# Attention with a state, then a Mish feed-forward layer: another order of loads, words and state products in the first of eight batches

## The chip, the cores and the metric

One core of a Trainium2 chip. The time is device microseconds of one execution; 706.59 us is the median of three runs. The engines are TensorE (PE), VectorE (DVE), ScalarE (ACT), GpSimd (POOL) and SyncE (SP); each runs its own instructions in order, and they wait for each other through semaphores. SP's instructions here are the issues of DMAs.

## The reference

Inputs: x of 8 batches x 8 heads x 512 tokens x 64, state of 8 x 8 x 32 x 64, and the layer's weights w_in (512 x 2048) and w_out (2048 x 512), both of them 64-bit floats in memory, two words of 32 bits for each value.

```python
scores = scale * x @ state.T            # per batch and head
a = softmax(scores); xread = a @ state
a2 = softmax(scale * state @ x.T); sread = a2 @ x
y = concat([xread, sread], axis=2)      # (8, 8, 544, 64)
y = y.transpose(0, 2, 1, 3).reshape(8 * 544, 512)
h = y @ w_in                            # (4352, 2048)
g = h * tanh(softplus(h))               # Mish
return g @ w_out                        # (4352, 512)
```

## The kernel before, in words

The rows of x are never multiplied by w_in as they stand. As xread is a @ state, the kernel forms state @ w_in for a batch (a *state product*, `sw_slice`, L351: 32 small matmuls for 128 columns), and multiplies the attention weights by that (the *first products*, `gemm1`, L387). Each float32 operand of a large matmul is split into a rounded high part and the rest (`hi`, `lo`; `swh`, `swl`; `gh`, `gl`), and three matmuls are done for one. Mish follows (`take_g`, L373), the split of its result (`split_g`, L377), and the *second products* with w_out (`gemm2`, L441), 24 matmuls of 128x128 by 512 columns, summed in four PSUM accumulators.

The work of a batch is cut into eight slots j = 0 to 7 (loop at L526), each with two 128-wide blocks of the 2048 columns. In slot j: first products j (12 matmuls), Mish j, the state product of slot j + 1, and the second products of an earlier slot, taken from the list `pending` by `second` (L522). Between these, pieces of the next batch's attention are taken from `todo` (L519).

Batch 0 has to bring the weights in as well. They are loaded in eight blocks each: `("i", e)` is block e of w_in, 1 MB in two DMAs (`load_w_in`, L96), `("o", j)` block j of w_out, also 1 MB in two (`load_w_out`, L114). All go through SP's queue, kept in the order of the calls by `load` (L473). A block of w_in waits for one of two raw buffers, which the join of the block before last frees; the load of x for batch 1 goes to the tile that holds x of batch 0 and waits for its last reader, `sread` (L303). The two words of each value are turned into a float32 in three steps: ACT scales the words (`scale_words`, L81: two instructions for w_in, one for w_out, where POOL does the other; block 0 of w_out has both on ACT), DVE joins them (`join_words`, L91), and for w_out DVE splits the result in high and low (`split_w_out`, L127). Mish and the function that scales the words (L87) lie in different tables of ACT, so that a table load of ACT stands between them.

The order on each engine is written down by hand with `behind` (L159): the instructions in the block come after the marked ones on the same engine, and on that engine only; where nothing is marked, a scheduler orders by its own estimate. The marks are entries of `last`, such as "PE", "words", "join", "mish", "swh", "swl". `fill` (L209) issues matmuls whose result nobody reads; each shows as two records in the profile. `FILL` (L28) holds three counts: ahead of state product 0 (L494), ahead of the transposes of the softmax (L502), and after state product 1 (L571).

In the rows, `wir` is a raw block of w_in, `wor` one of w_out, `swp` a state product, `ph` the first products, `acc` the second products (or, from L212, the filler), `ah` and `al` the split attention weights, `e` an exponential, `bd` a copy of the state blocks, `xTp` transposes of x.

Of the kernel before, what the change touches and what calls it, by code (L numbers as in the profile page):

```python
# [24 lines left out]
W = 1024  # L25
LAG = 2
WARM = 10
FILL = 24, 16, 4  # L28


def as_f32(ap):
    return ap.bitcast(F32)
# [7 lines left out]
def state_attention_mish_kernel(ctx, tc, x, state, w_in, w_out, out):  # L40

    nc = tc.nc
# [21 lines left out]
    wo = {}  # L64
# [16 lines left out]
    def scale_words(raw, pool_rounds=False):  # L81

        lw, hw = raw[..., 0], raw[..., 1]
        y = hw.bitcast(F32)
        if pool_rounds:
            nc.gpsimd.tensor_scalar(lw, lw, 0.876 * 2.0 ** -29, 0.49, ALU.mult, ALU.add)
        last["words"] = nc.scalar.activation(y, y, AF.Prelu, scale=2.0 ** -112, alpha=-2.0 ** 32)  # L87
        if not pool_rounds:
            last["words"] = nc.scalar.activation(lw, lw, AF.Copy, scale=0.876 * 2.0 ** -29, bias=0.49)  # L89

    def join_words(raw, to):  # L91
        lw, hw = raw[..., 0], raw[..., 1]
        last["join"] = nc.vector.scalar_tensor_tensor(
            to.bitcast(U32), hw, 3, lw, ALU.logical_shift_left, ALU.bitwise_or)
# [27 lines left out]
    def join_w_out(j, raw):  # L122
        w = pool.tile([P, 2, DM], F32, tag="wt", name=f"w_{j}", bufs=1)
        join_words(raw, w)
        return w

    def split_w_out(j, w):  # L127
        wo[j] = const.tile([P, 2, 2, DM], F32R, tag=f"wo{j}", name=f"wo_{j}")
        nc.vector.tensor_copy(wo[j][:, :, 1], w)
        last["wo"] = nc.vector.tensor_sub(wo[j][:, :, 0], w, as_f32(wo[j][:, :, 1]))  # L130
# [25 lines left out]
    last = {}  # L156

    @contextmanager
    def behind(*marks):  # L159

        with ExitStack() as st:
            for m in marks:
                st.enter_context(tc.issue_after(last[m].ins if hasattr(last[m], "ins") else last[m]))
            yield
# [10 lines left out]
    def attention(b, xs, sn):  # L175
# [75 lines left out]
        def wide(a):  # L251
            return a.unsqueeze(2).to_broadcast([P, 16, NS])

        def groups(a):
            return a.rearrange("p (g n) -> p g n", n=NS)
# [23 lines left out]
        def soft1_a():  # L279
            for kc in two:  # L280
                sm, r1 = small["s1"][kc], small["r1"][kc]
                nc.vector.tensor_reduce(sm, groups(e1[kc]), AX.X, ALU.add)
                nc.vector.tensor_scalar_add(sm, sm, 1e-9)
                nc.vector.reciprocal(r1, sm)
                nc.vector.tensor_mul(groups(e1[kc]), groups(e1[kc]), wide(r1))
            for kc in two:
                if b == 0:
                    at = ps_acc.tile([P, 512], F32, tag="acc", name=f"at_{b}_{kc}")
                    transposed(at, e1[kc])
                else:  # L290
                    at = temp(f"at_{b}_{kc}")
                    nc.vector.transpose(at, e1[kc])
                hi = pool.tile([P, S], F32R, tag=f"ah{kc}", name=f"ah_{b}_{kc}")
                lo = pool.tile([P, S], F32R, tag=f"al{kc}", name=f"al_{b}_{kc}")
                nc.scalar.copy(hi, at)
                last[b, "DVE"] = nc.vector.tensor_sub(lo, at, as_f32(hi))  # L296
                aT[kc] = (hi, lo)

# [28 lines left out]
        if b == 0:  # L327
            first = [lambda: (xt(0), xt(1), xt(2), xt(3), s_(), soft1_e()), soft1_a]
            fills.append(fill)
            rest = [  # L330
                lambda: (soft2_m(0), soft2_m(1)),
                lambda: (soft2_e(0), soft2_e(1)),
                lambda: (e2t(0), e2t(1)),
                lambda: (sr(0), sr(1)),
                lambda: sreadT(),
            ]
# [40 lines left out]
    def split_g(key, g):  # L377
        gh = pool.tile([P, W], F32R, tag="gh", name=f"gh_{key}")
        gl = pool.tile([P, W], F32R, tag="gl", name=f"gl_{key}")
        nc.vector.tensor_copy(gh, g)  # L380
        last["gl"] = nc.vector.tensor_sub(gl, g, as_f32(gh))  # L381
        return gh, gl
# [15 lines left out]
            phs.append(ph)  # L398
        return phs

    def mish(b, j, phs):
        g = new_g(f"{b}_{j}")
        for k, ph in enumerate(phs):
            take_g(g, k, ph)
        return split_g(f"{b}_{j}", g)


    def load_w_s(j):
# [61 lines left out]
    first, rest, aT = attention(0, xs0, sn0)  # L470
    raws, rawo = {}, {}

    def load(*what):  # L473
        for k, i in what:
            with behind("load"):
                if k == "i":
                    raws[i] = load_w_in(i)
                else:
                    rawo[i] = load_w_out(i)
# [5 lines left out]
            else:  # L485
                make_w_out(i, rawo.pop(i))

    load(("i", 0), ("o", 0), ("i", 1), ("o", 1))
    first[0]()
    with behind((0, "scs"), (0, "sub")):  # L490
        make(("i", 0))
    new_accs(0, NT)
    with behind("PE"):
        fills[0](FILL[0], accs[0][NT - 1])  # L494
    with behind((0, "exp")):
        scale_words(rawo[0])
    with behind("PE", "words"):
        sw_next = sw_slice(0, 0, P)
    with behind("swh"):
        scale_words(raws[1])  # L500
    with behind("PE"):
        fills[0](FILL[1], accs[0][NT - 1])  # L502
    with behind("PE", "words"):
        first[1]()
    load(("i", 2), ("o", 2), ("i", 3))
    with behind((0, "DVE")):
        join_w_in(1, raws.pop(1))
        w_0 = join_w_out(0, rawo[0])

    slots = []  # L510
    for b in range(B):
# [10 lines left out]
    def second(ts=None, keep=False):  # L522
        k_, fcs, g_, nt = pending[0] if keep else pending.pop(0)
        gemm2(k_, list(fcs), g_[0], g_[1], nt, ts)

    for n, (key, j) in enumerate(slots):  # L526
        if key == "s":
            if j == 0:
                ws_next = load_w_s(0)
            ws, ws_next = ws_next, load_w_s(j + 1) if j + 1 < 4 else None  # L530
            g = gemm1_s(j, ws)
            pending.append((key, (2 * j, 2 * j + 1, 2 * j + 8, 2 * j + 9), g, 2))
            second()
            continue
        if j == 0 and key > 0:
            aT = nxt_aT
        if key + 1 < B and j == (3 if key == 0 else 0):
            _, pcs, nxt_aT = attention(key + 1, xs_next, sn_next)
            todo += pcs
        phs = gemm1(key, j, aT, sw_next)  # L540
        if (key, j) == (0, 0):
            with behind("PE"):
                sw_next = sw_slice(0, 1, P)
            with behind("swl"):
                split_w_out(0, w_0)
            rawo.pop(0)
            with behind("swh", "wo"):
                g = mish(key, j, phs)
        else:
            g = mish(key, j, phs)  # L550
        pending.append((key, (j, j + 8), g, NT))
        if key == 0 and j + 1 < SLOTS:


            if j == 1:
                with behind("PE"):
                    second((0, 1), True)
            if j:
                with behind("PE"):
                    sw_next = sw_slice(0, j + 1, P)  # L560
            if j == 1:
                with behind("mish", "gl", "swh", "swl"):
                    rest[1]()
            with behind("mish", "gl", "swh", "swl", (0, "exp2") if j else "mish"):
                make(*makes.get(j, ()))
            if j == 0:
                with behind("join"):
                    rest[0]()
            if j == 0:
                with behind("PE"):  # L570
                    fills[0](FILL[2], accs[0][NT - 1])  # L571
                load(*((k, i) for i in range(3, 6) for k in "io" if (k, i) != ("i", 3)))
                with behind("load"):
                    xs_next, sn_next = load_x(1), load_state(1)
                load(*((k, i) for i in range(6, 8) for k in "io"))
            elif j == 1:
                with behind("PE"):
                    second((2, 3))
            elif j == 3:

                for do in (lambda: second((0, 1), True), todo.pop(0), lambda: second((2, 3))):
                    with behind("PE"):
                        do()
            elif j < 6:
                with behind("PE"):
                    second()
        else:
            nb, nj = (key, j + 1) if j + 1 < SLOTS else (key + 1, 0)
            if nb < B and nj % 2 == 0:
                sw_next = sw_slice(nb, nj)  # L590
        for _ in range((0, 0, 1, 1)[j] if key == 0 and j < 4 else 1 + (key == 0)):
            if todo:
                with behind(*(("PE",) if key == 0 and j == 2 else ())):
                    todo.pop(0)()
        if j == SLOTS - 1 and 0 < key + 2 < B:
            with behind("mish"):
                xs_next, sn_next = load_x(key + 2), load_state(key + 2)
        if len(pending) > LAG:
            second()
# [26 lines left out]
```

## Time and profile before

| | us |
|---|---|
| Median of three runs | 706.59 (706.54 to 710.52) |
| The profiled execution, whole | 707.5 |
| Its span, first to last instruction | 705.5 |
| PE busy in the span | 690.3 |
| ACT busy | 277.7 |
| DVE busy | 317.9 |

The span is what the profile's views cut up; the whole execution is 2.0 us longer, and 0.9 us above the median. An engine's busy time counts instructions that run, not those that wait; the idle time in brackets behind a row is the wait of that engine just ahead of it, and the arrow names what ended it.

### The profile page before, as it was taken

The numbers are of one execution on the slowest core, as the hardware profiler recorded it, in microseconds if no ns is written. First come the engines' busy times: TensorE is split into PE (matmuls) and PEld (weight loads), VectorE is DVE, ScalarE is ACT, GpSimd is POOL, SyncE is SP. The second block draws the span as 40 slices with busy tenths as digits, with TensorE's granted clock in tenths as the row PEclk, the third lists the DMA queues.
The fourth block names the chain that finished last, engine by engine and source line by source line (L and its number), as shares of the span: only waits on it lengthen the run. The fifth ranks groups of instructions, "written<-read, shape, count | busy, mean of one in ns | idle before, by whom it ended". The sixth has DMA issues, their size and how long they took to land.

```text
span 705.5 us, 11227 instructions
## 1 busy us (share of the span) xinstructions
PE 690.3 (98%) x4852; PEld 538.4 (76%) x4852; DVE 317.9 (45%) x493; ACT 277.7 (39%) x442; POOL 10.6 (1%) x13
## 2 busy tenths in 40 slices
PE   8889899999999999999999999999999999999997
PEld 7766676777777777777877777777777788977785
DVE  2697595283238323552346333732356324433221
ACT  5697755352236312551246123531247123222110
POOL 0111010000000000000000000000000000000000
PEclk9999999999999999999999999999999999999999
DMA  9997933000210011001010101001010007001001
GB/s 235 256 235 184 230 78 121 6 1 3 66 60 0 2 60 35 31 1 60 7 61 1 35 26 60 1 1 60 1 61 1 1 1 178 3 0 31 1 1 60
DMA packets 32305, 39.78 MB, mean 56 GB/s; under 512 B 5376, under 2 KB 25856, under 8 KB 32256
## 3 DMA queue, kind: packets, MB, share of 16 engines
q1 hardware_dynamic: 31824, 38.97, 21.1%
q8 instruction: 38, 0.62, 0.4%
q10 hardware_dynamic: 432, 0.10, 0.1%
q14 instruction: 11, 0.09, 0.0%
HBM read 25.95 MB, written 8.91 MB: 49 GB/s over the span
## 4 chain that ended last, share of the span: by engine, by line
PE 87%; DMA 5%; ACT 4%; DVE 3%; issue 1%; SPq 0%; ACTq 0%; DVEq 0%
PE acc L451 47%; PE ph L397 23%; PE swp L358 5%; DMA wir<-in_moe_w_in_dram 4%; PE ph_s L429 3%; PE acc_s L451 3%; PE xTp L184 2%; PE srp L308 1%; PE sc L197 1%; PE e2p L240 1%; DMA sn<-in_state_dram 1%; ACT wir L89 1%; ACT wor L87 1%; ACT L375 1%; ACT g L375 0%
## 5 line engine op out<-in xcount | busy, mean ns | idle before, releaser
L451 PE MATMUL acc<-wo,gh 128*128 128x512 f32 x1024 | 326.1, 400 | 0.0
L451 PEld LDWEIGHTS acc<-wo,gh 128*128 128x128 f32 x1024 | 188.4, 188 | 53.6 <-issue 13.5
L451 PE MATMUL acc<-wo,gl 128*128 128x512 f32 x512 | 200.8, 396 | 0.0
L375 ACT ACTIVATE g<-ph 128x512 f32<-128x512 f32 x128 | 74.3, 598 | 189.1 <-DVE gl L381 120.4
L380 DVE CAST gh<-g 128x1024 fp32r<-128x1024 f32 x64 | 44.9, 702 | 168.4 <-PE acc L451 144.9
L451 PEld LDWEIGHTS acc<-wo,gl 128*128 128x128 f32 x512 | 96.3, 188 | 23.2 <-issue 1.2
L397 PE MATMUL ph<-ah,swh 128*128 128x512 f32 x256 | 101.1, 396 | 3.2 <-ACT g L375 1.6
L397 PE MATMUL ph<-al,swh 128*128 128x512 f32 x256 | 101.8, 398 | 0.0
L397 PE MATMUL ph<-ah,swl 128*128 128x512 f32 x256 | 100.0, 393 | 0.0
L381 DVE TENSOR_TENSOR gl<-g,gh 128x1024 fp32r<-128x1024 f32 x64 | 78.3, 1224 | 4.8 <-DVE gh L380 0.5
L370 DVE TENSOR_TENSOR swl<-swp,swh 128x512 fp32r<-128x512 f32 (+1 forms) x72 | 43.0, 627 | 62.1 <-ACT swh L369 62.1
L397 PEld LDWEIGHTS ph<-ah,swh 128*128 128x128 f32 x256 | 48.0, 188 | 16.3 <-ACT g L375 1.8
L397 PEld LDWEIGHTS ph<-al,swh 128*128 128x128 f32 x256 | 48.1, 188 | 11.0 <-DVE al L296 0.4
L397 PEld LDWEIGHTS ph<-ah,swl 128*128 128x128 f32 x256 | 48.1, 188 | 10.0
L369 ACT CAST swh<-swp 128x512 fp32r<-128x512 f32 (+1 forms) x72 | 35.7, 545 | 25.9 <-PE swp L358 25.9
L358 PE MATMUL swp<-w_in_sb,bd 64*32 64x256 f32 (+1 forms) x1152 | 40.8, 358 | 2.1 <-DVE rs L229 2.0
L358 PEld LDWEIGHTS swp<-w_in_sb,bd 64*32 64x32 f32 x1152 | 18.5, 106 | 20.3 <-issue 10.6
L375 ACT ACT_TABLE_LOAD x20 | 25.7, 1283 | 14.9 <-DVE sm L227 6.2
L187 ACT COPY xT<-xTp 128x512 f32<-128x512 f32 x32 | 18.1, 590 | 33.5 <-PE xTp L184 33.2
L460 ACT COPY o<-acc 128x512 f32<-128x512 f32 x16 | 9.4, 587 | 44.8 <-PE acc L451 26.2
L426 DVE TENSOR_TENSOR wl<-ws,wh 128x512 fp32r<-128x512 f32 x16 | 11.1, 692 | 26.6 <-PE ph_s L429 19.8
L458 DVE COPY o<-acc 128x512 f32<-128x512 f32 x16 | 11.0, 688 | 26.4 <-DMA out_dram<-o 13.9
(79 smaller groups left out, 547.3 us busy)
## 6 DMA issues: line engine op xcount, KB each, us to landing
x<-in_x_dram SPq DMA_DIRECT2D x32, 256.0 KB, 3.7
wir<-in_moe_w_in_dram SPq DMA_DIRECT2D x16, 512.0 KB, 10.9
wor<-in_moe_w_out_dram SPq DMA_DIRECT2D x16, 512.0 KB, 13.7
out_dram<-o SPq DMA_DIRECT2D x32, 256.0 KB, 2.4
ws<-w_in_sb SPq DMA_DIRECT2D x16, 256.0 KB, 5.2
sn<-in_state_dram SPq DMA_DIRECT2D x21, 32.0 KB, 3.0
out_dram<-o_s SPq DMA_DIRECT2D x8, 64.0 KB, 1.8
sn<-in_state_dram ACTq DMA_DIRECT2D x3, 32.0 KB, 3.3
```

What stands on the lines that cost most here:

```text
L184: nc.tensor.transpose(pt[:, i * P:(i + 1) * P], xs[:, c, i // 2, (i % 2) * P:(i % 2 + 1) * P], ident)
L187: nc.scalar.copy(xTs[c], pt)
L358: last["PE"] = nc.tensor.matmul(pw[r][o, kc * n:(kc + 1) * n], bds[b][half(r), kc ^ r, o], w_in_sb[half(r), kc * NC + c, j * P:j * P + n], ...
L369: last["swh"] = nc.scalar.copy(hr, pr)
L370: last["swl"] = nc.vector.tensor_sub(lo[:, r].rearrange("p k f -> p (k f)"), pr, as_f32(hr))
L375: last["mish"] = nc.scalar.activation(g[:, k * 512:(k + 1) * 512], ph, AF.Mish)
L380: nc.vector.tensor_copy(gh, g)
L381: last["gl"] = nc.vector.tensor_sub(gl, g, as_f32(gh))
L397: last["PE"] = nc.tensor.matmul(ph, l, r, start=(i == 0), stop=(i == len(seq) - 1))
L426: nc.vector.tensor_sub(lo, w, as_f32(hi))
L429: nc.tensor.matmul(ph[r][:, k * 256:(k + 1) * 256], l[:, c], srT[i][:, c], start=(c == 0 and n == 0), stop=(c == NC - 1 and n == 2))
L451: last["PE"] = nc.tensor.matmul(accs[key][t], g[:, sl], wo[fc % 8][:, fc // 8, w, :], start=(fc == 0 and n == 0), stop=(fc == NFC - 1 and ...
```

## The change

Six edits, all of them in batch 0:

1. The fill counts go from 24, 16 and 4 to 12, 6 and 4.
2. The first loads go i0, i1, o0, o1 rather than i0, o0, i1, o1. Further on, x and state of batch 1 are loaded ahead of o5 rather than behind it.
3. ACT scales the words of o0 not ahead of state product 0 but behind the casts of the attention weights; DVE joins and splits o0 directly behind that.
4. In slot 0, Mish comes behind the words of o0 on ACT, and the casts of state product 1 come behind Mish; the split of Mish's result comes behind them. Before, the casts came first and then Mish.
5. In slots 2, 4, 5 and 6 the second products are cut in halves (tokens 0, 1 and 2, 3), with the state product between them, as in slots 1 and, in part, 3 before. Slot 6 now issues second products of its own.
6. In slot 1 the exponentials of the transposed softmax (`rest[1]`) come behind the words and joins of i3 and o2, not ahead of them.

```diff
-FILL = 24, 16, 4
+FILL = 12, 6, 4
...
-                nc.scalar.copy(hi, at)
+                last[b, "ACT"] = nc.scalar.copy(hi, at)
...
-    def mish(b, j, phs):
+    def take(b, j, phs):
         g = new_g(f"{b}_{j}")
         for k, ph in enumerate(phs):
             take_g(g, k, ph)
-        return split_g(f"{b}_{j}", g)
+        return g
...
-    load(("i", 0), ("o", 0), ("i", 1), ("o", 1))
+    load(("i", 0), ("i", 1), ("o", 0), ("o", 1))
...
-    with behind((0, "exp")):
-        scale_words(rawo[0])
-    with behind("PE", "words"):
+    with behind("PE", (0, "exp")):
         sw_next = sw_slice(0, 0, P)
...
-    with behind((0, "DVE")):
+    with behind((0, "ACT"), (0, "DVE")):
         join_w_in(1, raws.pop(1))
-        w_0 = join_w_out(0, rawo[0])
+        scale_words(rawo[0])
+        w_0 = join_w_out(0, rawo.pop(0))
+        split_w_out(0, w_0)
...
         if (key, j) == (0, 0):
-            with behind("PE"):
+            with behind("words"):
+                g_0 = take(key, j, phs)
+            with behind("PE", "mish", "wo"):
                 sw_next = sw_slice(0, 1, P)
             with behind("swl"):
-                split_w_out(0, w_0)
-            rawo.pop(0)
-            with behind("swh", "wo"):
-                g = mish(key, j, phs)
+                g = split_g(f"{key}_{j}", g_0)
         else:
-            g = mish(key, j, phs)
+            g = split_g(f"{key}_{j}", take(key, j, phs))
...
-            if j == 1:
+            if j and j != 3:
                 with behind("PE"):
                     second((0, 1), True)
...
-            if j == 1:
-                with behind("mish", "gl", "swh", "swl"):
-                    rest[1]()
-            with behind("mish", "gl", "swh", "swl", (0, "exp2") if j else "mish"):
+            with behind("mish", "gl", "swh", "swl"):
                 make(*makes.get(j, ()))
-            if j == 0:
-                with behind("join"):
-                    rest[0]()
+            if j < 2:
+                with behind("join", "words"):
+                    rest[j]()
...
-                load(*((k, i) for i in range(3, 6) for k in "io" if (k, i) != ("i", 3)))
+                load(("o", 3), ("i", 4), ("o", 4), ("i", 5))
                 with behind("load"):
                     xs_next, sn_next = load_x(1), load_state(1)
-                load(*((k, i) for i in range(6, 8) for k in "io"))
-            elif j == 1:
-                with behind("PE"):
-                    second((2, 3))
+                load(("o", 5), ("i", 6), ("o", 6), ("i", 7), ("o", 7))
...
-            elif j < 6:
+            else:
                 with behind("PE"):
-                    second()
+                    second((2, 3))
```

## Rows read from the trace of the kernel before

**Rows 1.** The page: its first part (busy time and share of the span of each engine, whole run) and, from its second part, the DMA engines' busy share in 40 slices of the span.

```profile
PE 690.3 (98%) x4852; PEld 538.4 (76%) x4852; DVE 317.9 (45%) x493; ACT 277.7 (39%) x442; POOL 10.6 (1%) x13
...
DMA  9997933000210011001010101001010007001001
```

**Rows 2.** The view: stretches of the span, in us. Columns: from:to and length, busy time (and instructions) of PE, PE's weight loads, DVE, ACT and POOL, then the granted TensorE clock, the DMA share and GB/s.

```profile
3.00:57.00 54.00, 48.62 (x438) 38.82 (x437) 37.47 (x53) 40.57 (x56) 5.65 (x4) 1.00 1.07 251
...
40.00:50.00 10.00, 7.98 (x65) 6.15 (x64) 9.26 (x15) 9.93 (x15) 2.26 (x1) 1.00 1.08 233
...
57.00:62.00 5.00, 5.00 (x82) 3.89 (x81) 2.02 (x5) 3.64 (x4) 1.12 (x1) 1.00 0.19 45
...
125.00:690.00 565.00, 565.00 (x3828) 441.29 (x3827) 232.09 (x367) 191.64 (x323) 0.00 (x0) 1.00 0.09 27
```

**Rows 3.** The view: TensorE's instructions from 0 to 125 us, grouped by line. Columns: line, engine, operation, tiles, shapes, count, busy us and mean ns, then the idle time ahead of them in us and what released them.

```profile
L397 PE MATMUL ph<-ah,swh 128*128 128x512 f32 x40 | 16.2, 409 | 3.2 <-ACT g L375 1.6 <-ACT swh L369 1.3 <-ACT ah L295 0.2
...
L212 PE MATMUL acc<-xT 128*128 128x128 f32 x88 | 10.5, 277 | 0.0
...
L358 PE MATMUL swp<-w_in_sb,bd 64*32 64x128 f32 (+1 forms) x288 | 8.7, 287 | 2.1 <-DVE rs L229 2.0
...
L184 PE MATMUL xTp<-ident,x 128*128 128x128 f32 x36 | 5.5, 280 | 2.0 <-DVE bd L151 1.6 <-ACT xT L187 0.2
```

**Rows 4.** The view: TensorE in order of time. Columns: start and length in us, engine, line, operation, tiles, shapes, count of records merged into the row, and in brackets the idle time ahead and its releaser.

```profile
1.36 4.64 PE L171 MATMUL warm<-ident 128*128 128x128 f32 x20 [1.36 <-POOL ident masks.py:199]
...
13.33 5.52 PE L212 MATMUL acc<-xT 128*128 128x128 f32 x48
...
19.38 3.84 PE L212 MATMUL acc<-xT 128*128 128x128 f32 x32
...
24.33 0.73 PE L397 MATMUL ph<-ah,swh 128*128 128x512 f32 x2 [0.24 <-ACT ah L295]
...
30.91 0.50 PE L397 MATMUL ph<-ah,swh 128*128 128x512 f32 x1 [1.61 <-ACT g L375]
...
36.67 0.67 PE L358 MATMUL swp<-w_in_sb,bd 64*32 64x128 f32 x32
...
45.09 0.67 PE L358 MATMUL swp<-w_in_sb,bd 64*32 64x128 f32 x32 [2.02 <-DVE rs L229]
...
51.37 0.39 PE L397 MATMUL ph<-ah,swh 128*128 128x512 f32 x1
...
55.14 0.69 PE L358 MATMUL swp<-w_in_sb,bd 64*32 64x128 f32 x32
...
67.61 0.50 PE L397 MATMUL ph<-ah,swh 128*128 128x512 f32 x1 [1.35 <-ACT swh L369]
...
94.59 0.67 PE L358 MATMUL swp<-w_in_sb,bd 64*32 64x128 f32 x32
```

**Rows 5.** The view: ScalarE and then VectorE in order of time, columns as in the group before.

```profile
12.34 1.16 ACT L87 ACTIVATE wir<-wir 128x1024 f32<-128x1024 f32 x1
...
21.19 1.16 ACT L87 ACTIVATE wir<-wir 128x1024 f32<-128x1024 f32 x1 [1.00 <-DMA wir<-in_moe_w_in_dram]
...
23.69 1.07 ACT L295 CAST ah<-at 128x512 fp32r<-128x512 f32 x2 [0.31 <-PE at L259]
...
28.30 0.65 ACT L369 CAST swh<-swp 128x256 fp32r<-128x256 f32 x2 [3.54 <-PE swp L358]
...
30.26 1.09 ACT L375 ACTIVATE g<-ph 128x512 f32<-128x512 f32 x2
...
41.55 1.15 ACT L87 ACTIVATE wir<-wir 128x1024 f32<-128x1024 f32 x1
...
58.35 1.28 ACT L87 ACT_TABLE_LOAD   x1 [1.44 <-DMA wir<-in_moe_w_in_dram]
...
74.28 1.15 ACT L87 ACTIVATE wir<-wir 128x1024 f32<-128x1024 f32 x1 [2.48 <-DMA wir<-in_moe_w_in_dram]
...
15.49 1.22 DVE L93 SCALAR_TENSOR_TENSOR w_in_sb<-wir 128x1024 uint32<-128x1024 uint32 x1
...
18.31 1.28 DVE L285 TENSOR_TENSOR e<-e,r 128x512 f32<-128x512 f32 x2
...
30.10 1.22 DVE L130 TENSOR_TENSOR wo<-w,wo 128x1024 fp32r<-128x1024 f32 x1
...
78.74 0.42 DVE L151 COPY bd<-st 128x256 f32<-128x256 f32 x1
...
87.40 1.25 DVE L93 SCALAR_TENSOR_TENSOR w_in_sb<-wir 128x1024 uint32<-128x1024 uint32 x1 [3.98 <-ACT wir L89]
```

**Rows 6.** The view: the loads. First three rows: SyncE's queue in order of time (start, length of the issue, both halves of a load together). Then two rows of the DMA issues, of the stretches 17.7 to 17.9 and 37.5 to 37.6 us, that is of the second halves of w_in's blocks 2 and 4 (tiles, queue, count, KB each, us from issue to landing). Last, one piece of the chain of work that ended last (start, length, what).

```profile
16.74 1.29 SPq L101 DMA_DIRECT2D wir<-in_moe_w_in_dram  x2
...
36.46 1.29 SPq L101 DMA_DIRECT2D wir<-in_moe_w_in_dram  x2
...
60.83 1.92 SPq L72 DMA_DIRECT2D x<-in_x_dram  x4
...
wir<-in_moe_w_in_dram SPq DMA_DIRECT2D x1, 512.0 KB, 12.4
...
wir<-in_moe_w_in_dram SPq DMA_DIRECT2D x1, 512.0 KB, 11.2
...
66.32 17.54 DMA wir<-in_moe_w_in_dram
```


## The prediction

> **What bounds the kernel now.** I read the page first, then stretches, then TensorE's waits, then each engine in order of time.
>
> The page shows TensorE (PE) busy for 98% of the span, and the DMA engines near full only in the first fifth [rows 1]. The table of stretches splits the run in two: from 125 to 690 us PE is busy for all of its 565 us, while from 3 to 57 us it is the DMA engines that are full (1.07 of their share) and PE has holes [rows 2]. So a microsecond of PE time saved before 110 us goes through to the end, and nothing else in this change can matter, since the diff touches batch 0 alone.
>
> What can be saved in the ramp is of two kinds. First, filler matmuls into a dead accumulator: 88 records, 10.5 us [rows 3], of which 48 run from 13.33 and 32 from 19.38, in 5.52 and 3.84 us [rows 4]. Second, waits of PE: 3.2 us ahead of the first products (`ph`), 2.1 us ahead of the state products (`swp`), 2.0 us ahead of the transposes of x, of which 1.8 us in batch 1 [rows 3]. The largest are 1.6 us at 30.91, 2.02 us at 45.09 and 1.35 us at 67.61 [rows 4].
>
> The floor under the ramp is the stream of weights. w_in word block i2 landed at 17.4 + 12.4 = 29.8 us, i4 at 37.1 + 11.2 = 48.3 (second halves; the issue is taken half a row after the pair's start), i5 at 58.33, where ScalarE (ACT) stopped waiting for it, and i7 at 66.32 + 17.54 = 83.9 [rows 5, 6]. i2 to i5 are 9.5 us per block. A slot of batch 0 costs PE about as much: 24 second products run from the state product at 45.09, which takes 0.6, to 51.37, so 5.7 us or 0.24 each; 12 first products of the same shape make 2.8, and all together 9.1 us [rows 4]. So PE has a small margin at best, and a shorter ramp soon runs into landings that don't move.
>
> **Loads, fills and the first slot.** Before, ACT's in-order stream is: words of i0, words of o0, casts of state product 0, then idle to 21.19 for i1, 2.2 us of i1 words, and only then the casts `ah` at 23.69, which the first product at 24.33 needs [rows 4, 5]. The fill of 32 covers that wait. With i1 second in the queue it lands after i0 alone: i0 was there by 12.34, and a block with its o partner takes about 9.5 us, so i1 comes between 12.3 + 4.5 = 16.8 and 18.2; I take 17.5. o0 then lands where i1 did, 21.2, since the bytes ahead are the same; o1 and i2 don't move.
>
> State product 0 needs only the join of i0, 15.49 + 1.2 = 16.7 [rows 5]; the fill of 12 calls is over at 13.33 + 24 x 0.115 = 16.1, so PE idles 0.6 us and does it 16.7 to 17.4 (before: 18.78). ACT casts it to 18.1, does i1's words to 20.3 (2 x 1.15, overlapped by 0.1) and `ah` to 21.3. VectorE (DVE) has the softmax scaled by 18.31 + 1.28 = 19.6, PE transposes at about 19.3 to 20.3, after 6 fill calls that end at 18.8. First product at about 21.0: a lead of 3.3 us (2.5 if i1 lands at 18.2, 3.9 at 16.8). PE's new idle time here is 0.6 + 0.5 + 0.7 = 1.8 us.
>
> The fills: 22 calls, or 44 records, go, 24 x 0.115 + 20 x 0.12 = 5.2 us of PE time. It isn't a gain by itself; it is what makes room for the lead.
>
> **Mish of slot 0.** Its ACT order is now: words of o0, Mish table load, Mish, casts of state product 1. Words of o0 run 21.3 to 23.5, the load 1.3 (the gap between 28.95 and 30.26), Mish 1.09, so Mish ends at 25.9 where it ended at 31.35, and the casts (0.65) at 26.6 [rows 5]. The join of i1 on DVE is done by 24.0, two joins (1.2 each) and the split of o0 (1.22 for its second half, and an estimated 0.7 for the cast ahead of it) by 26.9; `swl` follows. First products of slot 1 start at about 26.9 instead of 30.91: lead 4.0. This adds a wait: Mish now stands behind o0's landing. Behind it on ACT are Mish, both casts, and i2's words; on PE, slot 1. If o0 came 2 us late, all would be 2 us late, no more.
>
> **Slots 1 to 3.** i2 still lands at 29.8; words 2.15 and a join of 1.25 put it in place at 33.2. State product 2 stands between the halves of the second products, as before, and starts at 33.4 (before 36.67): lead 3.2, PE idle 0.6.
>
> Next the edit that I count on most. Before, PE idled 2.02 us at 45.09 for i3's join, because the two exponentials with their table load stood ahead of i3's words on ACT (41.55), and state product 3 stood ahead of all second products. Now i3's words come first and half of the second products stand ahead. i3 lands at about 39 (midway between i2 and i4), is joined by 42.4, and PE gets there at about 42.7: no wait. First products of slot 3 start at about 46.1 instead of 51.37: lead 5.3. The exponentials push Mish of slot 2 back, to about 44.6 to 45.7; its casts end at 46.3, just in time.
>
> State product 4 keeps its place right behind first product 3 (j = 3 is left out of the new order), with nothing to hide behind. PE is there at 49.7, but i4 lands at 48.3 and is in place at 48.3 + 2.15 + 1.25 = 51.7. PE idles 2.0 us and the lead falls to 55.14 - 51.7 = 3.4. This is the term that I trust most, since it hangs on a landing that the change can move by a few tenths only (the engines were full to 57 us).
>
> **Slots 4 to 7.** The 1.35 us at 67.61 came from state product 5 directly behind first product 4, waiting for Mish and casts; half of a second product on each side covers it now: lead 4.8. No wait needs i5 before 61.7, and PE asks at about 65.
>
> The load order matters here. SP issued o5 at 46.3, then stood until 60.83, since x of batch 1 goes into the tile that batch 0's last products with x must free [rows 6]; the DMA engines were at 0.19 of their share from 57 to 62 [rows 2]. Now o5 stands behind that x. With a lead of 3.4, x goes out at 57.4, so the hole in the stream stays about as wide; o5's 4.5 us (half of 9.5, rounded down) go behind it. i6 lands within a microsecond of the old time, and the old time is 74.2 (ACT waited for it 15.9 us after i5, before a table load that is gone). Its words and join end at about 78. PE reaches state product 6, with half a second product ahead of it, at about 77.5. That is half a microsecond of waiting.
>
> In between lie the transposes of batch 1's x: before, they waited 1.55 and 0.24 us, since DVE had the copy of the state blocks (78.74) queued behind the join of i6 [rows 3, 5]. If nothing changes, these 1.8 us stay and the lead is 4.8; if they go, it is 6.6 less the 0.5 above. The row says that DVE's order decides, and i6 lands no earlier, so I take the lower half: 5.3. i7 is in place at about 87.4 (landing 83.9, words, join; the table load is done while ACT waits) and PE asks at 88: no wait.
>
> I cost the rest at nothing: halving the second products of slots 2, 4, 5 and 6 issues the same 24 matmuls, and those of slot 5 only move from the next slot's end into slot 6; PE's full stretch hides either order, and if it didn't, a state product of 0.6 us per slot would be bare.
>
> **Sum.** Lead 3.3 at the first product, 4.0, 3.2, 5.3, 3.4, 4.8, and 5.3 us at 95 us, which the full PE carries to the end. Against this execution: span 705.5 - 5.3 = 700.2, time 707.5 - 5.3 = 702.2. The median of the runs is 0.9 us below the profiled one, so **701.3 us**. As a check by account: fills 5.2, old waits gone 0.24 + 1.6 + 2.0 + 1.35 = 5.2, new waits 1.8 + 0.8 + 0.6 + 2.0 = 5.2: 5.2 us left.
>
> **The clock.** Fewer fills leave PE idle for short times between 16 and 27 us. Row: the stretch of 40 to 50 us holds the wait of 2.02 us and its granted clock is 1.00, that is 2.4 GHz [rows 2]; no gap that I add is longer. The Trainium skill, "TensorE: Matmul & The Clock Gate", section "HAM oscillation", says that waits between bursts of matmuls can throw the array back to half its clock. By the rule the work after 20 us would run at half speed; by the row it does not. What this would cost, from rows: the matmuls at 1.36 us took 4.64 / 20 = 0.23 us each, the same shape in the fill 0.115. First products of slot 0 would take 6 us instead of 3.2, Mish would wait for them to 27, and the lead of slot 1 would fall from 4.0 to about 2. If it went on through slot 1, the rest goes too: 703 to 706.5.
>
> **Rivals.**
> - *Everything behind i4 closes up.* The 1.8 us of the x transposes go, i4 and i6 land half a microsecond earlier (SP can issue i3 and i4 some 3 us earlier, as buffers come free). Lead 3.9 + 1.35 + 1.8 = 7.1, or 8 if they come a microsecond and a half earlier: 698.6 to 699.5. For it: half a second product is a cover of 2.9 us. Against: full DMA engines. Chance 0.27.
> - *Joins hold the copy.* DVE and ACT stand in order behind i6, now behind o5 in the queue; the copy of the state blocks comes at 79 again and PE, early, waits longer for it. What is gained is then the half second product done ahead, 2.9 us: 703.7. For it: exactly this wait exists [rows 5]. Chance 0.16.
> - *The gate on x (slower).* SP's stand at x now holds o5, i6, o6, i7 and o7 rather than i6 on. i7 lands 83.9 - 60.8 + 4.5 = 27.6 us after x goes out and needs 4.7 to be in place (its join ended at 88.65) [rows 5, 6]. Before, state product 7 began at 94.6 [rows 4] with 10 of 24 second products done, by the order of the records; with 12 that is worth 95.1. So the change is slower than before once x goes out after 95.1 - 32.3 = 62.8 us, 2.0 us later than now, and each microsecond beyond costs one: at 66, 709.8. For it: nothing moves the transposed exponentials ahead, and they now stand behind the words of i3 and o2. Against: those end at 43.4, and PE asks for them at 47. Chance 0.05.
> - *The clock falls* as above: about 705. Chance 0.04.
> - The forecast itself: 0.48, between 699.8 and 703.
>
> **How the numbers follow.** The range goes from the closing-up case to the clock case: 697.5 to 705.8; outside are the slower gate and some luck. One per cent, 7.1 us, is about what a measurement here can tell from no change. Faster by more is the first rival, with a little of the forecast's edge: 0.29. Slower by more needs the gate and worse: 0.05. Within: 0.66.
>
> **What would show it.** In the profile after: first product 0 near 21 us; Mish of slot 0 near 25; no wait ahead of state product 3; a wait near 50 us ahead of state product 4 that ends with i4's join; x issued near 57; PE full from 95 us on; clock 1.00 throughout. I am wrong if i1 doesn't come before 19 us, if state product 4 doesn't wait, or if PE waits for i6 or i7 by microseconds.

## The result, and the profile after

| | before | changed |
|---|---|---|
| Median | 707.62 us (706.41 to 710.52, 6 runs) | 713.87 us (712.96 to 714.31, 6 runs) |
| Profiled execution, whole; its span | 707.5; 705.5 | 712.96; 711.1 |
| Mean granted clock of TensorE in it | 0.998 | 0.993 |

The ratio is 1.008, with a 95% interval of 1.0052 to 1.0109: slower by 0.8%, where 701.3 us was forecast and the range ended at 705.8. Of those 12.6 us, 1.0 is the median before, which was 706.59 over the first three runs. The page: TensorE's busy time shrank by 2.4 us (690.3 in [rows 1]), yet the span grew, and the DMA engines' first fifth has a hole in it.

```profile
PE 687.9 (97%) x4808; PEld 534.8 (75%) x4808; DVE 316.5 (45%) x493; ACT 276.8 (39%) x442; POOL 11.4 (2%) x13
...
PEclk9999899999999999999999999999999999999999
...
DMA  9995941200210010101010011001010006001001
```

TensorE in order of time, to be read against [rows 4]:

```profile
12.36 2.84 PE L212 MATMUL acc<-xT 128*128 128x128 f32 x24
...
15.89 0.67 PE L358 MATMUL swp<-w_in_sb,bd 64*32 64x128 f32 x32 [0.68 <-DVE w_in_sb L93]
...
19.88 0.73 PE L397 MATMUL ph<-ah,swh 128*128 128x512 f32 x2
...
25.50 0.50 PE L397 MATMUL ph<-ah,swh 128*128 128x512 f32 x1 [0.64 <-ACT swh L369]
...
34.43 0.67 PE L358 MATMUL swp<-w_in_sb,bd 64*32 64x128 f32 x32 [2.32 <-DVE w_in_sb L93]
...
43.58 0.67 PE L358 MATMUL swp<-w_in_sb,bd 64*32 64x128 f32 x32
...
51.01 0.66 PE L240 MATMUL e2p<-ident,e 128*128 128x128 f32 x4 [2.59 <-DVE swl L370]
...
55.09 0.64 PE L358 MATMUL swp<-w_in_sb,bd 64*32 64x128 f32 x16 [0.55 <-ACT e2T L242]
...
82.44 0.66 PE L184 MATMUL xTp<-ident,x 128*128 128x128 f32 x4 [3.79 <-ACT xT L187]
...
84.05 1.82 PE L358 MATMUL swp<-w_in_sb,bd 64*32 64x128 f32 x32
...
97.84 0.67 PE L358 MATMUL swp<-w_in_sb,bd 64*32 64x128 f32 x32
...
111.47 0.66 PE L240 MATMUL e2p<-ident,e 128*128 128x128 f32 x4 [1.61 <-ACT e L226]
...
122.28 0.50 PE L397 MATMUL ph<-ah,swh 128*128 128x512 f32 x1 [2.32 <-ACT swh L369]
```

To 30 us the forecast holds: first products at 19.88 (forecast 21.0, before 24.33; the start was 1.0 us earlier in this execution because the state landed sooner, which isn't of the change), those of slot 1 at 25.50 (26.9, before 30.91). The lead is 5.4 us. Then it goes: a wait of 2.32 us at 34.43, none at state product 3 (43.58, as forecast, where 2.02 us stood before), but 2.59 us at 51.01, inside the first products that follow. State product 4 begins where it did before (its first half at 53.90, its second at 55.09; the whole at 55.14 before), so the lead is gone ahead of x. Then come 3.79 us at the transposes of batch 1's x. State product 7 comes 3.2 us later than before.

ScalarE, against [rows 5]:

```profile
29.60 1.28 ACT L87 ACT_TABLE_LOAD   x1 [3.88 <-DMA wir<-in_moe_w_in_dram]
...
30.90 1.14 ACT L87 ACTIVATE wir<-wir 128x1024 f32<-128x1024 f32 x1
...
77.88 1.13 ACT L87 ACTIVATE wir<-wir 128x1024 f32<-128x1024 f32 x1 [4.04 <-DMA wir<-in_moe_w_in_dram]
...
80.02 1.28 ACT L375 ACT_TABLE_LOAD   x1
...
81.81 0.58 ACT L187 COPY xT<-xTp 128x512 f32<-128x512 f32 x1
...
121.15 0.58 ACT L460 COPY o<-acc 128x512 f32<-128x512 f32 x1 [3.47 <-DMA out_dram<-o]
```

i2's wait ends at 29.60, as forecast, but the table load runs after it, not during it. VectorE around the wait of 51 us:

```profile
46.93 0.69 DVE L380 CAST gh<-g 128x1024 fp32r<-128x1024 f32 x1 [2.25 <-ACT g L375]
...
49.40 1.22 DVE L130 TENSOR_TENSOR wo<-w,wo 128x1024 fp32r<-128x1024 f32 x1
...
50.54 0.75 DVE L370 TENSOR_TENSOR swl<-swp,swh 128x256 fp32r<-128x256 f32 x2
```

`swl` for slot 3 comes last there: Mish of slot 2 was late, since the exponentials now stand ahead of it on ACT, and the split of o2 stands ahead of `swl` on DVE.

SyncE's queue, then three pieces of the chain that ended last, against [rows 6]:

```profile
60.72 2.83 SPq L72 DMA_DIRECT2D x<-in_x_dram  x4
...
63.59 0.94 SPq L119 DMA_DIRECT2D wor<-in_moe_w_out_dram  x2
...
64.63 1.99 SPq L101 DMA_DIRECT2D wir<-in_moe_w_in_dram  x2
```

```profile
65.28 12.52 DMA wir<-in_moe_w_in_dram
...
85.87 5.24 PE acc L451 x12
...
95.11 2.80 PE acc L451 x12
```

x goes out at 60.72, 0.1 us earlier than before, with o5 now behind it and i6 behind that. The chain runs from x through SP to i6's DMA, ACT's words and table load, and the transposes at 83.42. Stretches, against [rows 2]:

```profile
57.00:62.00 5.00, 5.00 (x82) 3.94 (x81) 4.08 (x6) 3.75 (x4) 0.00 (x0) 1.00 0.06 9
...
78.00:84.00 6.00, 1.88 (x11) 1.03 (x9) 2.27 (x3) 5.83 (x8) 1.11 (x1) 0.99 1.10 232
...
84.00:90.00 6.00, 6.00 (x43) 4.49 (x43) 1.72 (x3) 4.09 (x6) 0.00 (x0) 0.50 1.06 241
```

From 57 to 62 us the DMA engines stand still (0.06, before 0.19). Behind the wait of 3.79 us the granted clock is 0.50, that is 1.2 GHz: 12 second products take 5.24 us at 85.87 and 2.80 at 95.11. With state product 6 (1.82 us at 84.05, before 1.39), the low clock costs 2.4 + 0.4 = 2.8 us, an estimate from these rows.

The account, after less before, in us of span: start -1.0; fills -4.9 (5.60 for 10.5 of [rows 3]); TensorE's waits from the first fill on +7.9 (15.6 for 7.7, by the idle times of its rows to 135 us); low clock +2.8. That makes 4.8 of the 5.6 us; 0.8 is not assigned.

### The profile page after: what moved, and what is told of

Read it like the earlier page. It is cut to its first block, busy times and chain, and to the rows that moved or that the text cites. A ratio compares the mean times of both kernels' runs of the same rounds, so it can differ in the third digit from the quotient of the medians.

```text
span 711.1 us, 11138 instructions
## 1 busy us (share of the span) xinstructions
PE 687.9 (97%) x4808; PEld 534.8 (75%) x4808; DVE 316.5 (45%) x493; ACT 276.8 (39%) x442; POOL 11.4 (2%) x13
## 4 chain that ended last, share of the span: by engine, by line
PE 89%; DMA 4%; ACT 3%; DVE 1%; issue 1%; SPq 1%; POOL 0%; ACTq 0%; POOLq 0%; DVEq 0%
PE acc L451 48%; PE ph L397 23%; PE swp L358 5%; DMA wir<-in_moe_w_in_dram 4%; PE ph_s L429 3%; PE acc_s L451 3%; PE xTp L184 2%; PE sc L197 1%; PE srp L308 1%; PE e2p L240 1%; DMA out_dram<-o 1%; ACT L375 1%; PE warm L171 1%; ACT g L375 0%; ACT wir L89 0%
## 5 line engine op out<-in xcount | busy, mean ns | idle before, releaser
L358 PE MATMUL swp<-w_in_sb,bd 64*32 64x256 f32 (+1 forms) x1152 | 40.3, 362 | 3.5 <-DVE w_in_sb L93 3.0
L358 PEld LDWEIGHTS swp<-w_in_sb,bd 64*32 64x32 f32 x1152 | 18.6, 107 | 21.6 <-issue 12.5
L272 DVE STREAM_TRANSPOSE e<-scs 128x512 f32<-128x512 f32 x14 | 9.1, 690 | 32.4 <-ACT scs L205 32.4
```

The source lines that it names most:

```text
L358: last["PE"] = nc.tensor.matmul(pw[r][o, kc * n:(kc + 1) * n], bds[b][half(r), kc ^ r, o], w_in_sb[half(r), kc * NC + c, j * P:j * P + n], ...
```

## The experiments

Theory from these rows: the loss is made at x. i6 and the transposes both hang on the moment when x leaves, so a lead doesn't shorten the wait there, and o5's place lengthens i6's way. Rivals: the later edits (halves, exponentials) cost it themselves; the clock does. Ratios are to the kernel before, run beside each, with 95% intervals. Rows come from one execution of each kernel, and those of one kernel differ by up to 9.5 us; where the profiled one lies at an end of that spread, its time is given.

**o5 ahead of x again.** 

> The changed kernel with one thing undone: o5 is loaded ahead of batch 1's x again. Theory (the gate on x): behind x, o5 makes i6 and i7 land some 3.5 us later (77.8 and 87.2 us instead of 74.2 and 83.9); ScalarE stands at i6's words, the copies of the x transposes stand behind them, TensorE waits 3.8 us and its clock then falls to 1.2 GHz for 6.8 us. Undone: i6 lands near 74, the wait at the x transposes shrinks to 1.5 us or less, the clock stays at 1.00, and the time is about 707 us (6 to 7 us below the changed kernel). Rival (the order on ScalarE and VectorE in slot 5 makes the wait, whatever lands): the wait and the low clock stay, 712 to 714 us.

```diff
-load(("o", 3), ("i", 4), ("o", 4), ("i", 5))
+load(("o", 3), ("i", 4), ("o", 4), ("i", 5), ("o", 5))
...
-load(("o", 5), ("i", 6), ("o", 6), ("i", 7), ("o", 7))
+load(("i", 6), ("o", 6), ("i", 7), ("o", 7))
```

712.48 us, 1.0058 (1.0032 to 1.0084). The rows (715.26 us, near its slowest):

```profile
61.75 3.08 SPq L72 DMA_DIRECT2D x<-in_x_dram  x4
```

```profile
75.33 1.28 ACT L87 ACT_TABLE_LOAD   x1 [4.65 <-DMA wir<-in_moe_w_in_dram]
...
78.67 1.11 ACT L87 ACTIVATE wor<-wor 128x1024 f32<-128x1024 f32 x1
```

```profile
82.32 2.45 PE L184 MATMUL xTp<-ident,x 128*128 128x128 f32 x12 [3.08 <-DVE bd L151]
```

i6 follows x by 13.6 us again (75.33 after 61.75), yet a wait of 3.08 us stays at 82.32, with a clock of 0.51 from 84 to 90 us, as the rival had it. ACT now has more to do behind i6's landing: a table load for its words, and words of w_out ahead of Mish, both of which came ahead of the landing in the changed kernel (70.64 and 72.70). Some 1.4 us came back, less than the intervals tell apart: o5's place alone is not the loss.

**The exponentials of slot 1 as before.** 

> The changed kernel with edit 6 undone: the two exponentials of slot 1 stand ahead of i3's words again. Theory (late Mish): in the changed kernel Mish of slot 2 stands behind words and exponentials, and the low part of state product 3 comes last on VectorE behind the split of o2, so TensorE waits 2.6 us inside first product 3. Undone: that wait goes or falls under 1 us; x of batch 1 goes out 1 to 2 us before 60.7; the late i6 stays, so the time is 710 to 712 us. Rival (neutral, the wait only moves to state product 3): 713 to 715 us.

```diff
+if j == 1:
+    with behind("mish", "gl", "swh", "swl"):
+        rest[1]()
-with behind("mish", "gl", "swh", "swl"):
+with behind("mish", "gl", "swh", "swl", (0, "exp2") if j else "mish"):
     make(*makes.get(j, ()))
...
-if j < 2:
-    with behind("join", "words"):
-        rest[j]()
+if j == 0:
+    with behind("join"):
+        rest[0]()
```

713.51 us, 1.0067 (1.0035 to 1.0099): no change that shows. Its profiled execution took 709.23 us, with 708.49 the fastest of ten, and is the forecast's own case: TensorE no longer waits for `swl` near 50 us, and x leaves at 57.80, within half a microsecond of the 57.4 forecast. Its SP, ACT and PE rows:

```profile
57.80 3.32 SPq L72 DMA_DIRECT2D x<-in_x_dram  x4
```

```profile
74.34 1.12 ACT L87 ACTIVATE wir<-wir 128x1024 f32<-128x1024 f32 x1 [3.98 <-DMA wir<-in_moe_w_in_dram]
```

```profile
78.89 0.66 PE L184 MATMUL xTp<-ident,x 128*128 128x128 f32 x4 [3.15 <-ACT xT L187]
```

i6 comes at 74.34, as forecast (74.2). TensorE, early, waits 3.15 us, and the clock from 80 to 88 us is 0.57.

**Slot 0 alone (edits 1 to 4 without the move of x).** The changed kernel with edits 5 and 6 undone and o5 ahead of x, the latter two as in the diffs above. 

> The kernel before with edits 1 to 4 alone (fills, i1 ahead of o0, o0's words later, Mish of slot 0 earlier); o5, halves and exponentials as before. Theory: the first product comes near 20.5 us and slot 1 near 26, but i2 lands at 29.6 as ever and its table load only starts then, so state product 2 comes near 34.4 and 2 us of lead are left, which reach the end: 704 to 705.5 us. Rival (the first slot is worth nothing because every later slot hangs on a landing): 706 to 708 us, and x of batch 1 goes out at 60.8 as before.

```diff
-if j and j != 3:
+if j == 1:
     with behind("PE"):
         second((0, 1), True)
...
-else:
+elif j == 1:
     with behind("PE"):
         second((2, 3))
+elif j < 6:
+    with behind("PE"):
+        second()
```

707.74 us, 0.9996 (0.9972 to 1.0021): no change, as the rival had it, though x left at 59.28. The lead of some 5 us is there at 25.57 and is eaten: 3.29 us of waiting at 34.70 with a granted clock of 0.72 behind it, 0.88 at 43.57, 1.34 at 66.06 and 1.67 at 77.77. So the first slot's edits are harmless and worthless as they stand.

**The table load ahead of i2's landing.** 

> The changed kernel with a one-column Prelu added ahead of the words of each block of w_in from i2 on, so that ScalarE's table load comes while it waits for the landing and not after it. Theory (the table load stands behind the landing): state product 2 comes 1.1 to 1.3 us earlier than 34.4, and each later wait on a landing loses as much; time 710 to 712.5 us. Rival (the load hides or the low part of a state product decides anyway): 713.5 to 715 us.

```diff
-scale_words(raw)
+if e >= 2:
+    tiny = pool.tile([P, 1], F32, tag="tiny", name=f"tiny_{e}")
+    last["tiny"] = nc.scalar.activation(tiny, ident[:, :1], AF.Prelu, scale=1.0, alpha=-1.0)
+    with behind("tiny"):
+        scale_words(raw)
+else:
+    scale_words(raw)
```

714.42 us, 1.0089 (1.0059 to 1.012). The wait at 34 us is gone (L364 is L358 here):

```profile
29.08 1.14 ACT L87 ACTIVATE wir<-wir 128x1024 f32<-128x1024 f32 x1 [1.30 <-DVE gh L386]
```

```profile
32.63 0.67 PE L364 MATMUL swp<-w_in_sb,bd 64*32 64x128 f32 x32
```

State product 2 comes 1.8 us earlier. The table load is 1.28 of that; in the rest i2's words also stopped waiting 0.5 us earlier (29.08 for 29.60). TensorE was ready 0.5 us later in this execution (32.63 for 34.43 - 2.32 = 32.11). So the table load made 1.3 of the 2.32 us. 2.09 us of waiting are left at 48.46 (2.59 in the changed kernel), and the transposes wait 4.67 us: nothing gained.

**Slot 0 alone, kept warm.** 

> The kernel of edits 1 to 4 alone, with 12 filler matmuls put into TensorE's stream just ahead of state product 2, where it waits 3.3 us for i2; they write an accumulator that is started afresh later. Theory (waits of TensorE cost twice, once as wait and once as a low clock behind it): the fillers end about when i2's join ends, the clock stays at 1.00 from 30 to 40 us (it was 0.83), and the median falls from 707.7 to 705 to 706 us. Rival (the low clock is only a mark of the runs, not a cost, or has another cause): 707.5 to 709 us.

```diff
+if j == 1:
+    with behind("PE"):
+        for _ in range(12):
+            last["PE"] = nc.tensor.matmul(
+                accs[0][NT - 1][:, :P], ident, ident, start=True, stop=True)
 if j:
     with behind("PE"):
         sw_next = sw_slice(0, j + 1, P)
```

706.62 us, 0.9983 (0.9957 to 1.0008). The fill takes the wait's place, and the clock behind it stays up, here against the same stretch without the fill:

```profile
34.00:40.00 6.00, 5.55 (x57) 4.18 (x57) 6.00 (x9) 5.96 (x11) 1.83 (x1) 1.00 1.07 272
```

```profile
34.00:40.00 6.00, 5.30 (x46) 4.19 (x47) 6.00 (x10) 5.94 (x12) 1.89 (x1) 0.72 1.07 253
```

That is 1.1 us in the median against slot 0 alone, well inside the intervals, and no clear gain over before.

**Halves alone (edit 5 on the kernel before).** 

> The kernel before with edit 5 alone: second products of slots 2, 4, 5 and 6 in halves around the state product. Theory (halves move work ahead of places where TensorE waits for something that comes no earlier, and change the order at the end of batch 0): waits of over 2 us near 80 and near 120 us, 709 to 712 us. Rival (they only reorder what is busy anyway): 707 to 708.5 us.

```diff
-if j == 1:
+if j and j != 3:
     with behind("PE"):
         second((0, 1), True)
...
-elif j == 1:
-    with behind("PE"):
-        second((2, 3))
...
-elif j < 6:
+else:
     with behind("PE"):
-        second()
+        second((2, 3))
```

708.61 us, 1.0011 (0.9987 to 1.0036): inconclusive. Waits of 1.63 us at 110.90 and 1.16 at 120.54 are there, as in the changed kernel, and one of 1.66 us at 51.57. At x, where the kernel before waited 1.55 us, the halves alone wait 2.71, as the theory had it, and the clock is 0.51 from 84 to 90 us:

```profile
61.29 1.92 SPq L72 DMA_DIRECT2D x<-in_x_dram  x4
```

```profile
74.39 1.28 ACT L87 ACT_TABLE_LOAD   x1 [4.17 <-DMA wir<-in_moe_w_in_dram]
```

```profile
81.48 1.09 PE L184 MATMUL xTp<-ident,x 128*128 128x128 f32 x8 [2.71 <-DVE bd L151]
```

**All late edits alone (5, 6 and the move of x).** The kernel before, with the halves of the last one and edit 6 as in the change. 

> The kernel before with edits 5, 6 and the move of o5 behind batch 1's x, and the first slot as before. Theory (the whole loss lies in the later slots): 712 to 715 us, with a wait of 3 us or more at the x transposes and a low clock behind it. Rival (the loss comes from the earlier first slot running into landings): 707 to 709.5 us.

```diff
-load(*((k, i) for i in range(3, 6) for k in "io" if (k, i) != ("i", 3)))
+load(("o", 3), ("i", 4), ("o", 4), ("i", 5))
...
-load(*((k, i) for i in range(6, 8) for k in "io"))
+load(("o", 5), ("i", 6), ("o", 6), ("i", 7), ("o", 7))
```

709.90 us, 1.0039 (1.0022 to 1.0056), between theory and rival: by the ratios the late edits cost 2.8 us by themselves and slot 0 gives 0.3, 2.5 together, while the change lost 5.7. Some 3 us exist only when both are there, barely clear of the intervals. Its rows at x (706.22 us, the fastest of twelve) show a shorter wait:

```profile
60.09 1.92 SPq L72 DMA_DIRECT2D x<-in_x_dram  x4
```

```profile
74.30 1.14 ACT L87 ACTIVATE wir<-wir 128x1024 f32<-128x1024 f32 x1 [2.84 <-DMA wir<-in_moe_w_in_dram]
```

```profile
78.88 0.66 PE L184 MATMUL xTp<-ident,x 128*128 128x128 f32 x4 [0.86 <-ACT xT L187]
```

**Second products whole.** Edit 5 undone in the changed kernel, as in the diff of slot 0 alone. 

> The changed kernel with edit 5 undone: second products of slots 2, 4, 5 and 6 whole, behind the state product. Theory (edit 5 made the waits of 1.6 us near 111 and 2.3 us near 122): these go back to 0.7 and 0, and the median falls to 709 to 711 us. Rival (the late i6 is what counts): 712.5 to 714.5 us.

```diff
-if j and j != 3:
+if j == 1:
     with behind("PE"):
         second((0, 1), True)
...
```

711.23 us, 1.0063 (1.0039 to 1.0087): below the changed kernel by 2.6 us in the medians, but by 1.2 in the ratios, whose intervals overlap, so the size is not settled. The wait near 122 us is gone, and that near 111 is 0.70 as before; 2.63 us come back at state product 3 and 2.60 stay at x.

**x behind i6.** 

> The changed kernel with one thing else: o5, i6 and o6 are loaded ahead of batch 1's x, so that only i7 and o7 stand behind SyncE's wait for the last use of x. Theory (i6 behind the gate makes the 3.8 us wait and the low clock behind it): i6 lands before 70 us, the wait at the x transposes falls under 1 us, no low clock from 80 to 91 us, median 706.5 to 709 us. Rival (the order on ScalarE and VectorE in slot 5 makes the wait whatever lands): the wait stays over 2.5 us, 711.5 to 714 us.

```diff
-load(("o", 3), ("i", 4), ("o", 4), ("i", 5))
+load(("o", 3), ("i", 4), ("o", 4), ("i", 5), ("o", 5), ("i", 6), ("o", 6))
...
-load(("o", 5), ("i", 6), ("o", 6), ("i", 7), ("o", 7))
+load(("i", 7), ("o", 7))
```

707.92 us, 0.9994 (0.9970 to 1.0017). This one edit of the changed kernel gives back 6 us, and its interval is clear of 1.0052. SP, PE and the stretches:

```profile
54.26 1.29 SPq L101 DMA_DIRECT2D wir<-in_moe_w_in_dram  x2
...
70.58 2.69 SPq L72 DMA_DIRECT2D x<-in_x_dram  x4
```

```profile
82.33 0.66 PE L184 MATMUL xTp<-ident,x 128*128 128x128 f32 x4 [0.24 <-ACT xT L187]
...
118.31 0.50 PE L397 MATMUL ph<-ah,swh 128*128 128x512 f32 x1 [2.17 <-ACT swh L369]
```

```profile
57.00:62.00 5.00, 5.00 (x61) 3.53 (x64) 3.71 (x5) 2.34 (x5) 0.23 (x1) 0.98 1.10 217
...
84.00:90.00 6.00, 6.00 (x63) 4.25 (x56) 2.61 (x4) 5.60 (x7) 1.11 (x1) 1.00 0.93 186
```

i6 is issued at 54.26 instead of 64.63, the DMA engines stay full from 57 to 62 us, the transposes wait 0.24 us, and the clock behind them is full. It is no faster than before: in these rows (710.61 us, the slowest of twelve) 3.28 us of waiting at 35.22 and 2.32 at 52.82, with the clock at 0.72 and 0.66 behind them (36 to 42, 53 to 58 us), and 2.17 at 118.31 eat the first slot's lead.

**Slot 0 kept warm, with that load order.** 

> Edits 1 to 4 alone, with 12 filler matmuls ahead of state product 2 and o5, i6, o6 ahead of batch 1's x. Theory: the wait of 1.0 to 1.7 us at the x transposes goes as well, every wait of TensorE stays under 1.5 us, clock 1.00 in nearly all runs: 704 to 706 us. Rival (i6 was not what that wait hung on): 706 to 708 us.

```diff
-load(("o", 3), ("i", 4), ("o", 4), ("i", 5), ("o", 5))
+load(("o", 3), ("i", 4), ("o", 4), ("i", 5), ("o", 5), ("i", 6), ("o", 6))
...
-load(("i", 6), ("o", 6), ("i", 7), ("o", 7))
+load(("i", 7), ("o", 7))
```

707.29 us, 0.9999 (0.9974 to 1.0024): a miss, though the wait at the transposes fell from 1.00 to 0.73 us. The wait at 65.23 (for DVE's `srd`) grew from 1.47 us to 2.03, with the clock at 0.72 from 66 to 72.

**No second products in slot 6.** 

> The changed kernel, but slot 6 issues no second products of its own, as before. Theory (slot 6 alone changes the order at the end of batch 0, so that ScalarE's output copies wait for the output's DMA with the casts of a state product behind them): the wait of 2.3 us near 122 goes and that near 111 falls to 0.7, median 710.5 to 712.5 us. Rival (the halves of slots 2, 4 and 5 do that): 713 to 715 us.

```diff
-if j and j != 3:
+if j in (1, 2, 4, 5):
...
-else:
+elif j < 6:
     with behind("PE"):
         second((2, 3))
```

718.04 us, 1.0149 (1.0121 to 1.0176): the theory that slot 6's share makes the late waits fell. They are 2.81 us at 115.90 and 1.92 at 127.82 without it. In span it is 5.5 us above the changed kernel. Its waits are 1.0 us more in all, and its clock is low in four stretches (0.72 from 34 to 40 us, 0.57 from 52 to 56, 0.62 from 84 to 92, 0.74 from 115 to 120) where the changed kernel has one; by estimate from these means, that is some 4 us. Why the clock fell there is open.

**Four edits together.** The changed kernel with x behind i6, the exponentials first, no second products in slot 6, and a fill ahead of state product 2; beside the diffs above, only the fill's count differs. 

> The changed kernel with all the repairs at once: o5, i6, o6 ahead of x, the exponentials of slot 1 ahead of i3's words, no second products in slot 6, and 9 filler matmuls ahead of state product 2. Theory (these four made the loss): no wait of TensorE over 1.5 us, clock 1.00, median 702.5 to 705 us. Rival (the loss sits in the halves themselves): 707 us or more.

```diff
-        for _ in range(12):
+        for _ in range(9):
```

709.20 us, 1.0029 (1.0007 to 1.0050): a miss again, in the rival's range. TensorE:

```profile
55.16 0.64 PE L358 MATMUL swp<-w_in_sb,bd 64*32 64x128 f32 x16 [1.75 <-ACT e2T L242]
...
108.94 0.66 PE L240 MATMUL e2p<-ident,e 128*128 128x128 f32 x4 [2.81 <-ACT e L226]
```

No kernel tried is faster than the one before beyond its interval.

## Why the prediction was wrong

**Right:** i1 second in the queue (words at 17.17 us), the first product, Mish and slot 1 about 5 us early, state product 3 without a wait, and a TensorE that is full from 125 us on.

**The step that failed** is the one on load order: "i6 lands within a microsecond of the old time", "half a microsecond of waiting" and, for the transposes of x, "I take the lower half: 5.3". TensorE waited 3.79 us there, and state product 7 came 3.2 us late. The distance from x to i6 was not the error: 74.2 - 57.4 = 16.8 us by the forecast, 17.16 in the changed kernel. The error is that the forecast let 4.8 to 5.3 us of lead pass an i6 that stays where it was. The transposes wait for ACT's copy `xT`, and that stands behind i6's words: an i6 at the old time puts them at the old time, 78.89 us with the exponentials first and 79.22 before. In the changed kernel x left at 60.72, with no lead left at all, and i6 came later by what o5 had added to its way.

The wait at x is the first two columns less the third; all are read off the rows (in us; for before, of the transposes at 79.22 with their 1.55), and what they tell is which column moved:

| | x to the end of ACT's wait for i6 | from there to the transposes | x to the moment TensorE asks | wait |
|---|---|---|---|---|
| before | 13.45 | 4.94 | 16.84 | 1.55 |
| changed | 17.16 | 4.56 | 17.93 | 3.79 |
| exponentials first | 16.54 | 4.55 | 17.94 | 3.15 |
| late edits alone | 14.21 | 4.58 | 17.93 | 0.86 |
| o5 ahead of x | 13.58 | 6.99 | 17.49 | 3.08 |
| halves alone | 13.10 | 7.09 | 17.48 | 2.71 |

x leaves when TensorE has done `sread`, so a lead at x moves all of these times together and is in none of the columns. With o5 behind x the first column grows; with the halves and o5 ahead of x the second does, as ACT then has the words' table load and words of w_out between i6's landing and the copy. So i6's distance is not the whole wait, and the order on ACT that edit 5 brought is the other part. Taking o5, i6 and o6 out from behind x made some 6 us come back. Why i6's distance differs by 3 us among kernels with one load order is open, and each figure is of one execution.

So the rival *Joins hold the copy*, to which I gave 0.16, had the mechanism at x, though in the changed kernel it is ACT's copy and not DVE's that comes last. Its price, 703.7, was too low, for it kept 2.9 us of lead and knew nothing of the clock. *The gate on x* had o5 in the right place, but looked at i7 and a late x; x left 2 us before its point of decision, and i6 was hit.

**Smaller terms.** The lead was also mis-sized ahead of x: 3.4 us forecast, 0.1 measured (60.72 for 60.83). i2's table load was costed at nothing ("words 2.15 and a join"), though a row of before shows it behind a landing, at 58.35 [rows 5]; state product 2 waited 2.32 rather than 0.6 us, and 1.3 of that is the table load. The exponentials were "just in time": 2.59 us of waiting came at 51.01, and went when they were put back. It went with edit 5 undone too, but then 2.63 us stood at state product 3, so the changed kernel had moved that wait rather than hidden it. The 2.0 us wait for i4, "the term that I trust most", didn't come, as TensorE was there only at 53.9.

**The clock** had 0.04 and a place at 16 to 27 us, where it stayed at 1.00 behind gaps of up to 0.7 us. It fell at 84 us, behind a wait I had priced at a half. In the same profile it stayed at 1.00 behind 2.32 and 2.59 us. By the Trainium skill, "TensorE: Matmul & The Clock Gate", section "HAM oscillation", a wait for a DMA between bursts of matmuls can send the array back to half clock; at x the trace agrees (0.50 behind 3.79 us). That section's case is no gap of half a microsecond, so my use of it at 16 to 27 us went beyond it. Nor did the price rest on a low clock: the matmuls at 1.36 us, at 0.23 us each, have a granted clock of 1.00 in the profile (1 to 6 us).

**Not foreseen:** waits of 1.61 and 2.32 us at 111 and 122 us, 3.2 us more than before. The second ends with `swh`, behind an output copy that waited 3.47 us for the output's DMA (ACT at 121.15). They belong to the halves of slots 2, 4 and 5, for they stand in every kernel with halves and in none without; why, no run shows. So edit 5, costed "at nothing", has waits of its own, and adds to the wait at x. By the ratios its whole price is 0.8 us (done alone) or 1.2 (undone; 2.6 by the medians), neither clear of the intervals.

## What to carry to other kernels

Ahead of a load that waits for an engine's own progress, put in the in-order queue all that this engine will need soon after; otherwise their distance behind the gate becomes a wait that no lead won earlier shortens. Before adding up leads, ask of each wait whether its releaser is tied to a landing that stands still or to the waiting engine's own past. Follow the waiting engine's order from the landing to the copy that is needed, table loads included. And price a wait of TensorE with the clock that may follow it.

## What was not expected of the hardware

- The table load of ACT stands behind the wait of the instruction that it serves: 29.60 us, 1.28 us long, right after a wait of 3.88 us; with another instruction of that table put ahead, it was gone from there.
- The clock does not fall behind every wait of a size (a mean between 0.5 and 1 is a stretch with both levels). Behind 1.75 us at 55.16 it was 0.57 (56 to 60 us, the last kernel), behind 2.03 us 0.72, behind 2.09 us 0.60 (50 to 54); behind 2.81 us at 108.94 it was 1.00 (110 to 116, the last kernel), behind 2.63 us at 43.04 also 1.00 (whole second products).
- It differs between executions of one kernel, and the time with it: slot 0 alone took 704.56 us at a mean clock of 1.000 and 711.78 at 0.990.
